# Third q loaded by a GpSimd gather, with eight of its rows loaded by SP

## The chip, the cores and the metric

The kernel runs on one core of a Trainium2 chip. The metric is device time in microseconds; three runs of the kernel before took 166.98 to 167.67 us, with a median of 167.11. One further execution was taken with the hardware profiler, and all rows of the profile are from that one.

## The reference

Linear attention with an ELU feature map, for 32 heads of 2048 rows by 128, all in bf16:

```python
phi_q = jnp.where(q > 0, q + 1, jnp.exp(q)) + 1e-6
phi_k = jnp.where(k > 0, k + 1, jnp.exp(k)) + 1e-6
kv = jnp.einsum("bhsd,bhse->bhde", phi_k, v)
z = jnp.einsum("bhsd->bhd", phi_k)
num = jnp.einsum("bhqd,bhde->bhqe", phi_q, kv)
den = jnp.einsum("bhqd,bhd->bhq", phi_q, z)[..., None] + 1e-6
return num / den
```

## The kernel before

The heads are worked through one after the other, each split into parts that overlap with those of its neighbours. A head's k, v and q are each one DMA of 512 KB: 128 partitions, each with 16 consecutive rows (4 KB, called a row of the transfer here). They land in rings of six buffers (`NBI`), and results leave from a ring of ten (`NBO`).

For each head, ACT takes exp of k, and POOL (DVE in the second head) takes relu of k. DVE clips the exp at 1 and adds the epsilon, so that phi is the sum of two tiles; both go into PE's products with v, or are added first for some of the 16 sub-tiles. PE accumulates kv with a column of ones for z. PE transposes q into PSUM, ACT and DVE take exp and relu of it from there, PE multiplies both with kv, and DVE divides and writes bf16. A store of 512 KB follows.

The first head's kv has no loop: PE runs warming products, the transposes of the first q, the first kv, the transposes of the second q and the first part of the second kv, and then enters a hardware loop of 5 turns of 6 heads.

The order on every engine is written out by hand: `Plan.add` (L32) takes an engine, a key and what an operation reads and writes, and an engine's operations are sorted by key (L57). Waits follow from reads and writes. Three rules touch this change:

- An operation that writes an entry waits for the entry's last writer if that is on another engine or is a DMA:

```python
            if w is not None and (w.eng != eng or w.dma):
                op.deps.append(w)
```

- A wait of an operation in PE's loop whose value is the same in every turn is asked once, ahead of the loop (L173 to L176, L195).
- SP's waits stand in its own order, so that what comes later on SP comes after them.

Loads are issued by SP (`load`, L376), with keys six heads ahead of use. The first ones are k0, q0, v0, k1, q1, v1, k2, q2, then a wait for v0, and k3, v2, k4, q3 and on. `late` (L597) gives the stores keys that move further behind the loads as the heads go on.

`SLOW` (L252) names one head, the fourth from the end, and partitions 16 to 19 and 48 to 51. That head's result is stored in two ways. POOL issues one indirect DMA with a list of row numbers (`row_sb`, made on DVE at L327 to L334); for those eight partitions the number is beyond the bound, so that they are left out. SP stores them as 3, 1, 3 and 1 rows (L604).

Of the kernel before, what the change touches and what calls it, by code (L numbers as in the profile page):

```python
# [6 lines left out]
ALU = mybir.AluOpType  # L7
P = 128
# [223 lines left out]
def bass_standalone__linear_attn_elu__prompt_kernel(  # L232
# [8 lines left out]
    NT = 16  # L241
    NH = B * H
    bf16 = mybir.dt.bfloat16
    fp32 = mybir.dt.float32
    NBI = 6
    NBO = 10
# [3 lines left out]
    HALF = NT * P // 2  # L250
    LAST = NH - 1
    SLOW = {LAST - 3: (16, 48)}  # L252

    ADD = (10, 11, 12, 13, 14)
    EVEN, ODD = tuple(range(0, NT, 2)), tuple(range(1, NT, 2))
# [4 lines left out]
    qf = q.rearrange("b h s d -> (b h) s d")  # L260
# [4 lines left out]
    with ExitStack() as es:  # L265
        def sb(name, shape, dt):
            return es.enter_context(nc.sbuf_tensor(name, shape, dt))
# [3 lines left out]
        q_sb = sb("q_sb", [P, NBI, NT * D], bf16)  # L271
# [10 lines left out]
        ident = sb("ident", [P, P], bf16)  # L282
        ones_sb = sb("ones_sb", [P, 1], bf16)
        first_sb = sb("first_sb", [1, 64], bf16)
        part_sb = sb("part_sb", [P, 1], mybir.dt.int32)
        off_sb = sb("off_sb", [P, len(SLOW)], fp32)
        num_sb = sb("num_sb", [P, len(SLOW)], fp32)
        row_sb = sb("row_sb", [P, len(SLOW)], mybir.dt.int32)

        xT_ps = es.enter_context(nc.psum_tensor("xT_ps", [P, NT * P], bf16))  # L290
        kvz_ps = es.enter_context(nc.psum_tensor("kvz_ps", [P, 512], fp32))
# [6 lines left out]
        def dma_sem(name):  # L298
            return dsems[name]

        for n, c in (("k", NBI), ("q", NBI), ("v", NBI), ("va", 1), ("o", NBO + 1 + len(SLOW))):
            for i in range(c):
                dsems[(n, i)] = es.enter_context(nc.semaphore(f"s_{n}{i}"))

        pl = Plan()

        def rows(x, h):
            return x[h].rearrange("(p j) d -> p (j d)", j=NT)
# [11 lines left out]
               reads=[("id0",)], writes=[("ident",)])  # L320
        pl.add("pool", -7, lambda g: g.memset(_ap(vfull, 0, [[VW, NBI], [1, GAP]]), 1.0), writes=[("vones",)])

        pl.add("pool", -6.9, lambda g: g.iota(part_sb[:], pattern=[[0, 1]], base=0, channel_multiplier=1), writes=[("part",)])
        for i, (h, groups) in enumerate(SLOW.items()):
            off, num, row = off_sb[:, i:i + 1], num_sb[:, i:i + 1], row_sb[:, i:i + 1]
            far = (groups[-1] - groups[0]) / 2
            steps = [lambda d, off=off, m=groups[0] + far + 1.5: d.tensor_scalar(off, part_sb[:], m, None, op0=ALU.subtract),  # L327
                     lambda d, off=off: d.tensor_tensor(out=off, in0=off, in1=off, op=ALU.mult)]
            if far:
                steps += [lambda d, off=off, m=far * far + 4.0: d.tensor_scalar(off, off, m, None, op0=ALU.subtract),  # L330
                          lambda d, off=off: d.tensor_tensor(out=off, in0=off, in1=off, op=ALU.mult)]
            steps += [lambda d, off=off, m=(3.5 * far) ** 2 + 4.0: d.tensor_scalar(off, off, m, float(NH * P), op0=ALU.is_lt, op1=ALU.mult),
                      lambda d, num=num, h=h: d.tensor_scalar(num, part_sb[:], float(h * P), None, op0=ALU.add),
                      lambda d, off=off, num=num, row=row: d.tensor_tensor(out=row, in0=num, in1=off, op=ALU.add)]  # L334
            for n, f in enumerate(steps):
                pl.add("dve", -8.3 + 0.01 * i + 0.001 * n, f, reads=[("part",)] + [("off", i)] * (n > 0), writes=[("off", i), ("row", i)])

        def mm_held(pe, out_ap, rhs, stop, start=False):
            return pe.add_instruction(mybir.InstMatmult(  # L339
                start_tensor_calc=start, stop_tensor_calc=stop, ldweights=False, bass_skip_group_check=True,  # L340
                tile_position=(0, 0), tile_size=(P, P), name=nc.get_next_instruction_name(), engine=mybir.EngineType.PE,
                ins=[pe.lower_ap(rhs), pe.lower_ap(held[0])], outs=[pe.lower_ap(out_ap)]))
# [27 lines left out]
        for h in range(NH):  # L370
# [3 lines left out]
            bi, b2, b3, bo = h % NBI, h % 2, h % 3, h % NBO  # L374

            def load(name, buf, src, key, h=h, bi=bi, after=()):  # L376
                dst, rws = buf[:, bi], rows(src, h)
                if name == "v":
                    dst = v_sb[:, bi, GAP:]
                return pl.add("sp", key, lambda sp: sp.dma_start(dst, rws), writes=[(name, bi)] + ([("vo", bi)] if name == "v" else []),  # L380
                              dma=(name, bi), after=after)
# [2 lines left out]
            this_v = load("v", v_sb, vf, h - NBI - 0.8)  # L384
            if h == 0:
                first_v.append(this_v)
            load("q", q_sb, qf, h - NBI - 0.9)

            pl.add("act", at("ek", -2.8),
                   lambda a, bi=bi, b2=b2: a.activation(ek_sb[:, b2, :], k_sb[:, bi, :], ACT.Exp),  # L390
                   reads=[("k", bi)], writes=[("ek", b2)])
# [8 lines left out]
            else:  # L400
# [4 lines left out]
                   reads=[("ek", b2)], writes=[("emk", b3)], kind="emk")  # L405
# [36 lines left out]
            if h:  # L442
                pl.add("pe", at("kv", -1.2), lambda pe, kv=kv, t=both_of: kv(pe, t, start=True),
                       reads=[("emk", b3), ("rk", b3, 0), ("rk", b3, 1)] + base, writes=[("bankkv",)])
            pl.add("pe", at("kv", -1.199), lambda pe, kv=kv, t=one_of, f=h == 0: kv(pe, t, start=f, stop=f),
                   reads=[("phix" if h == 1 else "phik", b3)] + base + ([] if h else [("first",)]), writes=[("bankkv",)])
            if h:
                pl.add("pool", h + 0.6, lambda g, bi=bi: g.memset(_ap(vfull, bi * VW + GAP + D - 1, [[2 * D, NT // 2], [1, 1]]), 1.0),
                       reads=[("v", bi)], writes=[("vo", bi)], kind="vo")
                pl.add("pe", at("kv2", -0.2985), lambda pe, kv=kv: kv(pe, ODD, stop=True),  # L450
                       reads=[("phik", b3), ("emk", b3), ("rk", b3, 0), ("rk", b3, 1), ("v", bi), ("vo", bi)], writes=[("bankkv",)])
            pl.add("act", at("kvs", -0.95), lambda a, b3=b3: a.activation(kvs_sb[:, b3, :], kvz_ps[:, 0:NC], ACT.Copy),  # L452
                   reads=[("bankkv",)], writes=[("kvs", b3)], kind="kvs")

            def tr(half, bi=bi):
                def f(pe):
                    for j in range(8 * half, 8 * half + 8):
                        last = pe.transpose(xT_ps[:, j * P:(j + 1) * P], q_sb[:, bi, j * P:(j + 1) * P], ident[:])  # L458
                    return last
                return f  # L460

            for half in (0, 1):
                pl.add("pe", h - 1.25 + 0.01 * half, tr(half), reads=[("q", bi), ("ident",)], writes=[("bankx", half)],
                       after=[halves[1]] if h == 1 and half == 0 else ())
            both = [("bankx", 0), ("bankx", 1)]

# [18 lines left out]
            else:  # L485
# [5 lines left out]
                   reads=[("eq", b2, 0), ("eq", b2, 1)], writes=[("emq", b3)], kind="emq")  # L491
# [105 lines left out]
            late = h + 1.0 + 0.18 * h  # L597
            if h in SLOW:
                i = list(SLOW).index(h)
# [3 lines left out]
                    reads=[("row", i)] + [("o", bo, p) for p in ("t", 0, 1, 2, 3, 4)], dma=("o", NBO + 1 + i))  # L603
# [38 lines left out]
```

## Time and profile before

| | |
|---|---|
| median of three runs | 167.11 us (166.98 to 167.67) |
| profiled execution | 167.06 us |
| its span, first to last instruction | 165.8 us |
| PE, DVE, ACT busy | 156.2, 153.2, 155.0 us |
| POOL busy | 107.6 us |
| DMA | 67.25 MB in 18605 packets, mean 406 GB/s |
| queue q1 (SP's) | 18448 packets, 66.63 MB |
| queue q0 (POOL's) | 144 packets, 0.49 MB |
| granted TensorE clock | 0.992 |

The page gives the busy time of each engine; the span cut into 40 slices of 4.15 us, each with a busy share in tenths; the DMA queues; and groups of instructions. A row of a timeline has start, length, engine, line and operation, and in brackets the idle time before it with what ended it. PEld is PE's weight load, SPq an issue on SP's queue. An issue's landing is the time at which all 16 DMA engines have counted its semaphore up.

### The profile page before, as it was taken

How to read it: one execution, taken by the hardware profiler on the slowest of the kernel's cores; microseconds unless marked ns; L12 is line 12 of the kernel's file. 1: busy time of each engine (PE TensorE's matmuls, PEld its weight loads, DVE VectorE, ACT ScalarE, POOL GpSimd, SP SyncE). 2: the span in 40 equal slices, each digit the busy share in tenths (PEclk: the TensorE clock that was granted, in tenths of full speed). 3: DMA queues.
4: the chain of work that ended last, by engine and by line, in shares of the span. 5: the costliest groups of instructions: out<-in, count | busy, mean ns of one | idle time of the engine just before them, and what ended most of it. 6: DMA issues, size and time to landing. Idle time of an engine off the chain costs nothing.

```text
span 165.8 us, 6280 instructions
## 1 busy us (share of the span) xinstructions
PE 156.2 (94%) x2819; PEld 145.7 (88%) x2453; DVE 153.2 (92%) x277; ACT 155.0 (94%) x143; POOL 107.6 (65%) x130
## 2 busy tenths in 40 slices
PE   7799999999999999999999999999999999999970
PEld 0379899999999999899999989999998999999960
DVE  3588999999999999999999999999999999999992
ACT  3989999999999999999999999999999999999681
POOL 2406688776767887676778767676887767678510
PEclk9999999999999999999999999999999999999996
DMA  5999999999999999999999999999999999999986
GB/s 192 409 416 420 414 421 414 397 390 407 421 417 422 416 420 420 419 420 416 420 419 420 418 421 416 419 420 420 418 420 419 421 419 420 418 419 419 418 348 259
DMA packets 18605, 67.25 MB, mean 406 GB/s; under 512 B 2082, under 2 KB 2210, under 8 KB 18594
## 3 DMA queue, kind: packets, MB, share of 16 engines
q1 hardware_dynamic: 18448, 66.63, 99.2%
q0 software_dynamic: 144, 0.49, 0.7%
q8 instruction: 5, 0.08, 0.2%
q14 instruction: 6, 0.05, 0.1%
q10 hardware_dynamic: 2, 0.00, 0.0%
HBM read 50.33 MB, written 16.81 MB: 405 GB/s over the span
## 4 chain that ended last, share of the span: by engine, by line
DVE 59%; PE 17%; POOL 12%; ACT 6%; issue 3%; DMA 2%; DVEq 0%
DVE o_sb L546 20%; POOL rk_sb L412 12%; DVE rq_sb L478 11%; DVE emk_sb L404 10%; DVE emq_sb L490 10%; PE kvz_ps L435 6%; PE o_ps L505 5%; PE o_ps L506 5%; ACT ek_sb L390 3%; DVE rden_sb L534 3%; DVE o_sb L539 3%; ACT eq_sb L469 2%; DMA k_sb<-in_k_dram 2%; DVE den_sb L528 2%; DVE rk_sb L412 1%
## 5 line engine op out<-in xcount | busy, mean ns | idle before, releaser
L435 PE MATMUL kvz_ps<-v_sb,rk_sb 128*128 128x129 bf16 (+1 forms) x512 | 67.0, 220 | 2.9 <-POOL rk_sb L412 1.2
L546 DVE TENSOR_TENSOR o_sb<-o_ps,rden_sb 128x768 bf16<-128x768 f32 (+2 forms) x62 | 67.9, 1135 | 0.0
L412 POOL TENSOR_TENSOR rk_sb<-rk_sb,emk_sb 128x640 bf16<-128x640 bf16 x30 | 41.9, 1396 | 39.6 <-DVE emq_sb L490 38.3
L394 POOL TENSOR_SCALAR rk_sb<-k_sb 128x1024 bf16<-128x1024 bf16 (+1 forms) x60 | 64.1, 1069 | 2.5 <-DMA k_sb<-in_k_dram 2.5
L505 PE MATMUL o_ps<-kvs_sb,emq_sb 128*128 128x129 bf16 (+1 forms) x536 | 65.2, 217 | 0.0
L506 PE MATMUL o_ps<-kvs_sb,rq_sb 128*128 128x129 bf16 (+1 forms) x536 | 64.4, 217 | 0.0
L469 ACT ACTIVATE eq_sb<-xT_ps 128x2048 bf16<-128x2048 bf16 (+1 forms) x33 | 60.1, 1823 | 2.7 <-PE xT_ps L458 2.7
L390 ACT ACTIVATE ek_sb<-k_sb 128x2048 bf16<-128x2048 bf16 x32 | 61.0, 1908 | 1.6 <-DMA k_sb<-in_k_dram 1.6
L435 PE MATMUL kvz_ps<-v_sb,emk_sb 128*128 128x129 bf16 (+1 forms) x338 | 53.3, 221 | 0.0
L435 PEld LDWEIGHTS kvz_ps<-v_sb,rk_sb 128*128 128x128 bf16 x512 | 46.1, 98 | 7.7 <-POOL rk_sb L412 3.1
L505 PEld LDWEIGHTS o_ps<-kvs_sb,emq_sb 128*128 128x128 bf16 x536 | 51.2, 98 | 0.8 <-issue 0.5
L506 PEld LDWEIGHTS o_ps<-kvs_sb,rq_sb 128*128 128x128 bf16 x536 | 51.3, 98 | 0.0
L458 PE MATMUL xT_ps<-ident,q_sb 128*128 128x128 bf16 x512 | 34.1, 220 | 0.5 <-DMA q_sb<-in_q_dram 0.5
L458 PEld LDWEIGHTS xT_ps<-ident,q_sb 128*128 128x128 bf16 x512 | 30.2, 98 | 4.8 <-DMA q_sb<-in_q_dram 4.3
L435 PEld LDWEIGHTS kvz_ps<-v_sb,emk_sb 128*128 128x128 bf16 x338 | 32.5, 98 | 0.3 <-DVE emk_sb L404 0.2
L339 PE MATMUL kvz_ps<-ones_sb,rk_sb 128*128 128x1 bf16 x232 | 31.3, 165 | 0.0
L476 ACT ACTIVATE rq_sb<-xT_ps 128x1024 bf16<-128x1024 bf16 x30 | 30.9, 1031 | 0.0
L404 DVE TENSOR_SCALAR emk_sb<-ek_sb 128x2048 bf16<-128x2048 bf16 x32 | 22.0, 689 | 3.0 <-ACT ek_sb L390 3.0
L478 DVE TENSOR_SCALAR rq_sb<-xT_ps 128x1024 bf16<-128x1024 bf16 x34 | 23.3, 689 | 1.5 <-ACT eq_sb L469 1.5
L490 DVE TENSOR_SCALAR emq_sb<-eq_sb 128x2048 bf16<-128x2048 bf16 x32 | 21.9, 684 | 0.0
L339 PE MATMUL kvz_ps<-ones_sb,emk_sb 128*128 128x1 bf16 x121 | 19.9, 166 | 0.0
L452 ACT ACTIVATE kvs_sb<-kvz_ps 128x129 bf16<-128x129 f32 x32 | 9.0, 282 | 1.5 <-PE kvz_ps L435 0.9
(37 smaller groups left out, 51.6 us busy)
## 6 DMA issues: line engine op xcount, KB each, us to landing
k_sb<-in_k_dram SPq DMA_DIRECT2D x32, 512.0 KB, 14.9
q_sb<-in_q_dram SPq DMA_DIRECT2D x32, 512.0 KB, 15.1
v_sb<-in_v_dram SPq DMA_DIRECT2D x32, 512.0 KB, 15.1
out_dram<-o_sb SPq DMA_DIRECT2D x30, 512.0 KB, 15.4
out_dram<-o_sb SPq DMA_DIRECT2D x1, 288.0 KB, 3.3
out_dram<-o_sb SPq DMA_DIRECT2D x1, 224.0 KB, 3.1
out_dram<-o_sb SPq DMA_DIRECT2D x2, 12.0 KB
out_dram<-o_sb SPq DMA_DIRECT2D x2, 4.0 KB
```

What stands on the lines that cost most here:

```text
L339: return pe.add_instruction(mybir.InstMatmult(start_tensor_calc=start, stop_tensor_calc=stop, ldweights=False, bass_skip_group_check=True, ...
L390: lambda a, bi=bi, b2=b2: a.activation(ek_sb[:, b2, :], k_sb[:, bi, :], ACT.Exp),
L394: pl.add(eng, key, lambda e: e.tensor_scalar(rk_sb[:, b3, c], k_sb[:, bi, c], BIG, 0.0, op0=ALU.min, op1=ALU.max), reads=[("k", bi)] + ([( ...
L404: lambda d, b2=b2, b3=b3: d.tensor_scalar(emk_sb[:, b3, :], ek_sb[:, b2, :], 1.0, EPS, op0=ALU.min, op1=ALU.add),
L412: return e.tensor_tensor(out=a, in0=a, in1=b, op=ALU.add)
L435: last = pe.matmul(kvz_ps[:, 1 - l:NC], lhsT=w, rhs=v_sb[:, bi, c - l:c + D], start=first, stop=fin, skip_group_check=True)
L458: last = pe.transpose(xT_ps[:, j * P:(j + 1) * P], q_sb[:, bi, j * P:(j + 1) * P], ident[:])
L469: halves[part] = pl.add("act", key, lambda a: a.activation(eq_sb[:, b2, c], xT_ps[:, c], ACT.Exp), reads=both[part:part + 1] or both, writ ...
L478: f = lambda d: d.tensor_scalar(rq_sb[:, b3, c], xT_ps[:, c], 0.0, None, op0=ALU.max)
L505: pe.matmul(o_ap, lhsT=emq_sb[:, b3, t * P:(t + 1) * P], rhs=kvs_sb[:, b3, c0:c1], start=True, stop=False)
L506: return pe.matmul(o_ap, lhsT=rq_sb[:, b3, t * P:(t + 1) * P], rhs=kvs_sb[:, b3, c0:c1], start=False, stop=True)
L546: pl.add("dve", key, lambda d: d.tensor_tensor(out=o_sb[:, bo, 3 * g0:3 * g1, :].rearrange("p (a b) d -> p a b d", b=3), in0=_ap(full, bas ...
```

## The change

The third head's q (`EARLY = 2`) is no longer one DMA on SP. SP loads its partitions 16 to 18, 19, and 48 to 51 as three DMAs, with a key that puts them ahead of the second q. POOL then issues one indirect DMA that gathers the other 120 rows by a list. The list is the scatter's, moved by a whole number of heads with one more operation on DVE, so that the eight rows stay out of bounds. The gather waits for the three loads; the transposes of the third q, and of every later q in the same buffer, also read the gather's entry `qa`.

```diff
+    EARLY = 2
...
-        row_sb = sb("row_sb", [P, len(SLOW)], mybir.dt.int32)
+        row_sb = sb("row_sb", [P, len(SLOW) + 1], mybir.dt.int32)
...
+        first = next(iter(SLOW))
+        pl.add("dve", -8.2, lambda d: d.tensor_scalar(row_sb[:, len(SLOW):len(SLOW) + 1], row_sb[:, 0:1], float((EARLY - first) * P), None, op0=ALU.add),
+               reads=[("row", 0)], writes=[("row", len(SLOW))])
...
-            load("q", q_sb, qf, h - NBI - 0.9)
+            if h == EARLY:
+                few = []
+                for p0, p1 in ((SLOW[first][0], SLOW[first][0] + 3), (SLOW[first][0] + 3, SLOW[first][0] + 4), (SLOW[first][1], SLOW[first][1] + 4)):
+                    few.append(pl.add("sp", 0.05 - NBI, lambda sp, p0=p0, p1=p1, bi=bi, h=h: sp.dma_start(q_sb[p0:p1, bi], rows(qf, h)[p0:p1]),
+                           writes=[("q", bi)], dma=("q", bi)))
+                pl.add("pool", 0.5, lambda g, bi=bi: g.indirect_dma_start(
+                    q_sb[:, bi], None, q.rearrange("b h (p j) d -> (b h p) (j d)", j=NT),
+                    bass.IndirectOffsetOnAxis(ap=row_sb[:, len(SLOW):len(SLOW) + 1], axis=0), bounds_check=NH * P - 1, oob_is_err=False),
+                    reads=[("row", len(SLOW))], writes=[("qa", bi)], dma=("qa", 0), after=few)
+            else:
+                load("q", q_sb, qf, h - NBI - 0.9)
...
-                pl.add("pe", h - 1.25 + 0.01 * half, tr(half), reads=[("q", bi), ("ident",)], writes=[("bankx", half)],
+                pl.add("pe", h - 1.25 + 0.01 * half, tr(half), reads=[("q", bi), ("ident",)] + [("qa", bi)] * (bi == EARLY), writes=[("bankx", half)],
```

More of the change, by code (lines that the diff above doesn't have):

```diff
@@ L299, in dma_sem @@
             return dsems[name]
-        for n, c in (("k", NBI), ("q", NBI), ("v", NBI), ("va", 1), ("o", NBO + 1 + len(SLOW))):
+        for n, c in (("k", NBI), ("q", NBI), ("v", NBI), ("va", 1), ("qa", 1), ("o", NBO + 1 + len(SLOW))):
             for i in range(c):
```

## The prediction

> **What bounds the kernel now.** I read the page's parts 1 to 3 first, then the stages, then the first 17 us on SP, PE and ACT, and last the completion records of the stores.
>
> Part 1 has PE, DVE and ACT at 92 to 94%. Part 2 has the DMA engines as full as they are:
>
> ```profile
> DMA  5999999999999999999999999999999999999986
> GB/s 192 409 416 420 414 421 414 397 390 407 421 417 422 416 420 420 419 420 416 420 419 420 418 421 416 419 420 420 418 420 419 421 419 420 418 419 419 418 348 259
> ```
>
> After the first slice they never rest. The stage table (columns: stage, length, busy time with count of PE, PEld, DVE, ACT, POOL, granted clock, DMA share, GB/s) says the same and shows where the share falls:
>
> ```profile
> 80.00:120.00 40.00, 39.55 (x742) 38.38 (x652) 39.30 (x68) 39.58 (x36) 28.95 (x35) 1.00 1.03 419
> 120.00:156.00 36.00, 35.48 (x669) 34.34 (x578) 35.30 (x62) 34.05 (x29) 25.55 (x29) 1.00 1.03 419
> 156.00:160.00 4.00, 3.88 (x72) 3.71 (x71) 3.86 (x9) 3.71 (x11) 1.27 (x2) 1.00 1.01 407
> 160.00:162.00 2.00, 0.78 (x14) 0.60 (x11) 1.90 (x10) 1.87 (x8) 0.00 (x0) 1.00 0.75 299
> ```
>
> 67.25 MB at 419 GB/s are 160.5 us of a 165.8 us span. So there are two bounds side by side: the chain of engines, and the DMA engines. Which ends last is read from the final store, issued at 162.57. Its 16 completion counts (one for each DMA engine, from the trace's completion records) land at 164.45 to 164.62 for twelve engines, then 164.88, 165.22, 165.47 and 165.72. The twelve had run dry and waited for compute (the 0.75 above); the last four still had a backlog. The span ends with the last of them. **An idle stretch of a backlogged DMA engine therefore lengthens the kernel one for one.** Compute has 1.1 us to spare there (165.72 less 164.62).
>
> **What the change does at the start.** Issues of SP in before, with time, length and operation:
>
> ```profile
> 0.74 0.38 SPq L380 DMA_DIRECT2D k_sb<-in_k_dram  x1
> 1.18 0.42 SPq L380 DMA_DIRECT2D q_sb<-in_q_dram  x1
> 1.65 0.42 SPq L380 DMA_DIRECT2D v_sb<-in_v_dram  x1
> 2.12 0.43 SPq L380 DMA_DIRECT2D k_sb<-in_k_dram  x1
> 2.59 0.49 SPq L380 DMA_DIRECT2D q_sb<-in_q_dram  x1
> ...
> 4.09 0.45 SPq L380 DMA_DIRECT2D q_sb<-in_q_dram  x1
> 6.97 0.33 SPq L380 DMA_DIRECT2D k_sb<-in_k_dram  x1
> ```
>
> Eight loads are queued by 4.5 us. By issue-to-landing times of 3.4, 4.2, 5.3, 6.1 and 6.9 us the first five land at 4.1, 5.4, 7.0, 8.2 and 9.5: in order of issue, 1.25 us apart. That queue covers the wait for the first v that ends at 6.97.
>
> In the changed program the fifth to seventh issues are the 3, 1 and 4 rows. All three write the same buffer entry, and the planner makes a DMA that writes what another DMA wrote wait for it (L44 to L48). Its listing of SP has that wait ahead of the 1 row and ahead of the 4 rows; the second q (L385) comes after them:
>
> ```
> 3 L385 DMACopy k_sb<-in_k_dram 128x2048
> 4 L395 DMACopy q_sb<-in_q_dram 3x2048
> 5 L395 DMACopy q_sb<-in_q_dram 1x2048 [waits s_q2]
> 6 L395 DMACopy q_sb<-in_q_dram 4x2048 [waits s_q2]
> 7 L385 DMACopy q_sb<-in_q_dram 128x2048
> ```
>
> So SP stands still twice, and the second q, second v, third k and all later loads are behind it.
>
> **The sum, step by step.**
> 1. The 3 rows are issued at 2.59, behind the second k, whose counts land from 7.67 to 8.2. One row more on three engines takes 0.16 us (1.25 us for 8 rows): 7.8 to 8.4, taken 8.0. SP wakes within 0.02 (v at 6.95, issue at 6.97).
> 2. The 1 row is issued at 8.02, when the queue has just run dry (the 512th row ends at 7.51 in the packet records). No row shows one 4 KB row from an empty queue. Below: the 64 bytes that ACT loads (issue 0.74, landing 1.91), 1.17 us. Above: the first k, 3.40 us for 8 rows an engine, less 1.25 for the rows: 2.15. I take 1.6, near the middle, since the row is a single packet but as far from a warm queue as the first k: 9.6.
> 3. The 4 rows are issued at 9.62 without holding the second q, which goes one issue pitch (0.47) later: 10.1, between 9.5 and 11.05 by the bounds above.
> 4. The second q lands after 3.40 us at most (the first k's own time) and 2.42 at least (1.17 + 1.25). Taken 2.9: 13.0 instead of 9.45. **The DMA stream is 3.55 us late**, with ends 2.4 and 5.0.
>
> The Trainium skill (DMA: Bandwidth & Descriptors, Anatomy of one DMA) puts a fixed cost of about 2.0 us on a DMA, mostly the receipt of the last write, fitted on GpSimd's path. The trace's smallest load shows 1.17. By the page step 2 would end 0.4 later and the time be 170.8, an estimate that the sum does not use.
>
> Beside this the other edits are small:
> - The list: one more 128x1 operation on DVE. Its kin take 0.15 to 0.16 us at 1.8 to 3.1 us, and DVE idles until 6.11: nothing. Without that cover it costs 0.2.
> - The relief: 8 rows leave one DMA engine. That rows 16 to 19 and 48 to 51 are one engine's is borne out at the end of before: the slowest count is 1.7 us behind the next (161.88 and 160.20) for the store ahead of the scatter that leaves those rows out, and 0.25 behind (165.72 and 165.47) after it. 8 rows are 1.25 us, but the next engine ends 0.25 earlier, so **the relief is worth 0.25**, unless that next engine gets the extra row of L395 (0.09 then).
> - The gather on POOL: POOL waits for the three loads, issues, and then does the memset that waited until 12.42 in before. Its issue is bounded by the scatter's 1.14 us. POOL's relu for the third head, behind it in the queue, waits for the third k anyway and has 1.3 us of idle after it.
> - PE: the changed listing asks for the gather at the loop's entry, ahead of the first numerators, not ahead of the third transposes. In before PE enters at 12.2. What is queued behind: numerators, the rest of kv, and the transposes that ACT's exp at 16.67 waits for.
>
> ```profile
> 10.05 1.05 PE L458 MATMUL xT_ps<-ident,q_sb 128*128 128x128 bf16 x16
> 11.14 1.88 ACT L469 ACTIVATE eq_sb<-xT_ps 128x2048 bf16<-128x2048 bf16 x1 [0.82 <-PE xT_ps L458]
> 12.91 1.90 ACT L390 ACTIVATE ek_sb<-k_sb 128x2048 bf16<-128x2048 bf16 x1
> ```
>
> Compute moves too: the second transposes start at 13.0 instead of 10.05, so the exp behind them (ACT idles only 0.82 ahead of it) is 2.9 late. The gather: the 4 rows land near 11.2, and the scatter's landing took 3.9 (first engine) to 6.5 us (last), so PE enters at 15.1 to 17.7. From entry to the third exp PE needs 3.7 us, and 16.67 - 3.7 is 12.95, or 12.8 through ACT's chain: compute is 2.3 to 4.9 late. Steady rounds have DVE at 98% and give nothing back. Compute decides the end only above 3.55 - 0.25 + 1.1 = 4.4, so the DMA stream is the later one.
>
> Sum: 3.55 - 0.25 = **+3.3 us**, span 165.8 to 169.1. The profiled execution took 167.06, which is 1.3 over its span and 0.05 under the median of 167.11. **Forecast 170.4 us.**
>
> **Rivals.**
> - *The gather decides.* Where it lands 6.5 us after its issue, PE enters at 17.7, compute is 4.9 late and the last counts land at 164.62 + 4.9 = 169.5: 170.9 us. DVE is busy from 9.2 to 11.9 in before; if POOL cannot write its list of transfers beside it, 0.7 to 1.0 more, 171.9. The Trainium skill states such a lock (SBUF — State Buffer, SBUF: two separate sides); the scatter's 1.14 us beside a DVE relu of 0.68 does not show it. Against: the 6.5 belongs to an engine 2 us behind, and none is so late at 11 us. Chance 0.20.
> - *Compute hides part.* If the late engines catch up (the 0.75 at 160 to 162 shows that most can), compute alone decides, 3.0 late: 164.62 + 3.0 = 167.6, or 169.0 us. Against: four engines never ran dry. Chance 0.14.
> - *Not slower.* If the small loads landed under cover of queued loads, with the second q issued before 6.6 (7.5 less 0.9 to the first packet), only the relief would stay: 166.8 us. For: they use 1 to 4 engines. Against: loads land in order of issue, and the small stores of the end, issued from 152.1, landed at 158.3 to 158.8, behind the store issued before them. Chance 0.04.
>
> The forecast itself has 0.60, and 0.02 is left for what I have not thought of.
>
> **The numbers.** Range: 2.4 and 5.0 less 0.25, so 169.2 to 171.8; this holds the gather's case at 170.9 and leaves out part of the second rival. A measurement of this kernel tells 0.5% (0.84 us) from no change. Slower by more: 0.95; within: 0.03; faster: 0.02, all from the last rival and the rest.
>
> **What would show it.** SP: 3 rows near 2.6, 1 row near 8.0, 4 rows near 9.6, the second q near 10.1, with two waits for q_sb of some 5 and 1.6 us. The third slice of GB/s falls from 416 to about 150. PE waits for q_sb at the second transposes, to about 13. The gather's issue stands near 11.2. In the final store the slowest count is no longer alone. I am wrong if SP issues the second q before 6.6, if the third slice stays near 400, or if PE's wait at the loop's entry runs past 17.2: then the gather decides.

## The result, and the profile after

| | before | changed |
|---|---|---|
| time, median of 6 runs each on the same chip, us | 167.29 (166.98 to 168.57) | 175.58 (175.29 to 176.98) |
| ratio | | 1.0498, 95% interval [1.0448, 1.0548] |
| profiled execution: time, span, us | 167.06, 165.8 | 175.82, 174.5 |

The change makes the kernel slower by 8.3 us. The forecast was 170.4 with a range to 171.8: the direction is right, the size is not.

Part 2 of the changed kernel's page first (40 slices of 4.4 us; the clock that TensorE was granted, the DMA engines' busy tenths, GB/s):

```profile
PEclk9996579999999999999999999999999999999999
DMA  5659999999999999999999999999999999999356
GB/s 215 269 185 394 412 416 417 415 362 416 414 417 420 419 420 419 418 418 420 418 420 421 420 419 419 417 418 420 420 421 420 420 421 420 421 417 416 127 229 250
```

Two things are to be seen besides the hole of the third slice, which the forecast expected (185; it said about 150). The clock falls to 0.5 in the fifth slice. And the last three slices are no longer full: in before the DMA engines were busy to the end, here they run dry from about 162 us on. The end has changed hands, from DMA to the engines.

SP's rows answer to those of before, then POOL's row with the gather, and the landing of the two indirect DMAs (last column: us from issue to landing):

```profile
2.59 7.12 SPq L395 DMA_DIRECT2D q_sb<-in_q_dram  x3
9.76 0.36 SPq L385 DMA_DIRECT2D q_sb<-in_q_dram  x1
```

```profile
12.28 1.20 POOL L397 DMA_INDIRECT q_sb<-in_q_dram,row_sb  x1 [6.36 <-issue]
```

```profile
q_sb<-in_q_dram,row_sb POOLq DMA_INDIRECT x1, 8.6
out_dram<-o_sb,row_sb POOLq DMA_INDIRECT x1, 5.1
```

The three small loads hold SP until the second q goes out at 9.76 (forecast 10.1); by the completion records it lands at 12.99 (forecast 13.0). So SP's part came as worked out. The gather did not: the last small rows land at 11.27, POOL issues 1.0 us after that, and the rows need 8.6 us, longer than any scatter here does (at most 7.4, in experiment 11). What this does to PE, in its waits and at the row where it enters the loop:

```profile
PE o_ps L520 <- DMA q_sb<-in_q_dram,row_sb: 5.3, 1, 5.3
```

```profile
21.06 0.28 PE L520 MATMUL o_ps<-kvs_sb,emq_sb 128*128 128x129 bf16 x1 [5.29 <-DMA q_sb<-in_q_dram,row_sb]
```

In before PE did not wait there:

```profile
12.22 0.22 PE L505 MATMUL o_ps<-kvs_sb,emq_sb 128*128 128x129 bf16 x1
```

So the first numerator (a product of the first q with kv) starts 8.8 us later than in before. ACT shows what follows. Its rows for the second head's kvs (kv as ACT copies it out of PSUM), the exp of the fourth k and the exp of the third q, in before and then in the changed kernel:

```profile
14.71 0.27 ACT L452 ACTIVATE kvs_sb<-kvz_ps 128x129 bf16<-128x129 f32 x1
14.87 1.91 ACT L390 ACTIVATE ek_sb<-k_sb 128x2048 bf16<-128x2048 bf16 x1
16.67 1.88 ACT L469 ACTIVATE eq_sb<-xT_ps 128x2048 bf16<-128x2048 bf16 x1
```

```profile
24.31 0.28 ACT L467 ACTIVATE kvs_sb<-kvz_ps 128x129 bf16<-128x129 f32 x1 [5.65 <-PE kvz_ps L450]
24.49 1.90 ACT L405 ACTIVATE ek_sb<-k_sb 128x2048 bf16<-128x2048 bf16 x1
26.30 1.88 ACT L484 ACTIVATE eq_sb<-xT_ps 128x2048 bf16<-128x2048 bf16 x1
```

Compute is 9.6 us late here, and 9.75 at the last DVE operation, which ends at 172.29 instead of 162.54 (before, then changed):

```profile
161.99 0.55 DVE L546 TENSOR_TENSOR o_sb<-o_ps,rden_sb 128x384 bf16<-128x384 f32 x1
```

```profile
171.74 0.55 DVE L561 TENSOR_TENSOR o_sb<-o_ps,rden_sb 128x384 bf16<-128x384 f32 x1
```

The span grows by 8.7, as about 1 us comes back at the end: all 16 counts of the last store land together, 174.22 to 174.44, without the backlog that put the last one at 165.72 in before. The stages show where PE stood and how it came back (length, busy time with count of PE, PEld, DVE, ACT, POOL, granted clock, DMA share, GB/s):

```profile
12.00:16.00 4.00, 2.48 (x34) 2.11 (x26) 0.00 (x0) 1.83 (x1) 1.33 (x2) 0.76 1.00 397
16.00:20.00 4.00, 0.00 (x0) 0.00 (x0) 3.70 (x4) 1.95 (x2) 1.95 (x2) 0.50 1.01 404
20.00:24.00 4.00, 2.94 (x30) 2.95 (x31) 0.00 (x0) 0.00 (x0) 2.33 (x2) 0.50 1.03 421
...
160.00:164.00 4.00, 4.00 (x78) 3.90 (x69) 3.94 (x7) 2.69 (x3) 2.66 (x5) 1.00 0.70 277
```

From 16 to 20 PE does nothing at all, and from 21 to 24 it works at half clock. It was not the wait for the gather that brought the clock down: by the trace's clock record it is 0.50 from 14.06 to 24.30, so it fell before that wait began (15.78), after PE had stood from 10.02 to 13.08 for the second q. The long wait kept it down. At 160 to 164 PE and DVE are full and the DMA share is 0.70.

One figure worked out from the packets helps with all that follows: the **stream's lag**, how much later than in before the DMA engines have moved as many bytes. In the changed kernel it is 4.1 us at 20 us and 4.2 us at 40, 80, 120 and 155 us. So the forecast's stall is there, 4.2 us for 3.55, and stays. But the end is 8.7 us late, and it is not the stream that ends last.

### The profile page after: what moved, and what is told of

Same layout as the page of the kernel before. It is cut to its first block, busy times and chain, and to the rows that moved or that the text cites. A ratio compares the mean times of both kernels' runs of the same rounds, so it can differ in the third digit from the quotient of the medians.

```text
span 174.5 us, 6293 instructions
## 1 busy us (share of the span) xinstructions
PE 157.2 (90%) x2819; PEld 147.2 (84%) x2453; DVE 154.5 (89%) x278; ACT 155.2 (89%) x143; POOL 108.7 (62%) x131
## 4 chain that ended last, share of the span: by engine, by line
DVE 56%; PE 17%; POOL 11%; DMA 10%; issue 3%; SPq 1%; POOLq 0%
DVE o_sb L561 20%; POOL rk_sb L427 11%; DVE rq_sb L493 10%; DVE emq_sb L505 9%; DVE emk_sb L419 9%; PE kvz_ps L450 6%; PE o_ps L520 6%; PE o_ps L521 5%; DMA q_sb<-in_q_dram 5%; DMA q_sb<-in_q_dram,row_sb 5%; DVE rden_sb L549 3%; DVE o_sb L554 3%; DVE den_sb L543 2%; SPq L385 1%; PE kvz_ps L344 0%
## 5 line engine op out<-in xcount | busy, mean ns | idle before, releaser
L520 PE MATMUL o_ps<-kvs_sb,emq_sb 128*128 128x129 bf16 (+1 forms) x536 | 66.1, 219 | 5.3 <-DMA q_sb<-in_q_dram,row_sb 5.3
L450 PE MATMUL kvz_ps<-v_sb,rk_sb 128*128 128x129 bf16 (+1 forms) x512 | 67.9, 223 | 2.6 <-DVE rk_sb L427 0.8
L521 PE MATMUL o_ps<-kvs_sb,rq_sb 128*128 128x129 bf16 (+1 forms) x536 | 65.1, 219 | 0.0
L450 PE MATMUL kvz_ps<-v_sb,emk_sb 128*128 128x129 bf16 (+1 forms) x338 | 54.0, 223 | 0.2 <-issue 0.2
L450 PEld LDWEIGHTS kvz_ps<-v_sb,rk_sb 128*128 128x128 bf16 x512 | 46.8, 99 | 7.2 <-POOL rk_sb L427 2.6
L505 DVE TENSOR_SCALAR emq_sb<-eq_sb 128x2048 bf16<-128x2048 bf16 x32 | 23.1, 721 | 0.0
```

Source lines behind the costliest of these rows:

```text
L450: last = pe.matmul(kvz_ps[:, 1 - l:NC], lhsT=w, rhs=v_sb[:, bi, c - l:c + D], start=first, stop=fin, skip_group_check=True)
L505: lambda d, b2=b2, b3=b3: d.tensor_scalar(emq_sb[:, b3, :], eq_sb[:, b2, :], 1.0, EPS, op0=ALU.min, op1=ALU.add),
L520: pe.matmul(o_ap, lhsT=emq_sb[:, b3, t * P:(t + 1) * P], rhs=kvs_sb[:, b3, c0:c1], start=True, stop=False)
L521: return pe.matmul(o_ap, lhsT=rq_sb[:, b3, t * P:(t + 1) * P], rhs=kvs_sb[:, b3, c0:c1], start=False, stop=True)
```

## The experiments

Theory A is the forecast's: SP stands still, the DMA stream is late, and the late stream sets the end. Theory B: the gather's landing sets it, through PE's wait at the loop's entry and the half clock after it; SP's stall lies beneath. Every kernel here is the changed one with the edit shown, unless said otherwise.

**1. No chain** (the three loads count on semaphores of their own).

```diff
+                    own = ("qs", len(few) - 1) if few else ("q", bi)
-                           writes=[("q", bi)], dma=("q", bi)))
+                           writes=[own], dma=own))
```

> The three small loads count on semaphores of their own, so that SP issues them one behind the other and waits for none; the gather still waits for all three. Theory A, the forecast's: SP's stall is what costs, the second q lands at about 10 us instead of 12.99 and nearly all of the loss is gone, about 168 us. Theory B: the end is set by the gather's last landing at PE's loop entry and by the half clock behind it. Its issue moves from 12.3 to about 9.4 to 10 us, its last landing from 20.8 to about 17.5 to 18.5, PE's first numerator from 21.1 to about 18 to 18.7, and the time falls by the same 2.5 to 3 us, to about 172.5 to 173 us.

174.01 us, ratio 1.0396 [1.0357, 1.0435]. SP, POOL and PE:

```profile
2.59 0.93 SPq L396 DMA_DIRECT2D q_sb<-in_q_dram  x3
```

```profile
11.28 1.20 POOL L398 DMA_INDIRECT q_sb<-in_q_dram,row_sb  x1 [5.10 <-DMA q_sb<-in_q_dram]
```

```profile
19.32 0.28 PE L521 MATMUL o_ps<-kvs_sb,emq_sb 128*128 128x129 bf16 x1 [5.78 <-DMA q_sb<-in_q_dram,row_sb]
```

SP waits for nothing, the stream's lag falls to 0.2 us, and still 6.4 us of loss remain: **theory A falls.** PE enters 7.1 us late and the span (172.8) is 7.0 us longer. B was 1.0 to 1.5 us too hopeful: the gather is issued at 11.28, not 9.4 to 10. The small rows queue behind the first four loads, the last of which lands at 9.43, and their own last count is at 10.29; POOL takes another 1.0 us from there to the issue.

**2. Chain only** (the whole third q by SP, no gather).

```diff
-                pl.add("pool", 0.5, lambda g, bi=bi: g.indirect_dma_start(
...
+                load("q", q_sb, qf, h - NBI - 0.9)
```

> The three small loads and SP's two waits stay, the gather is gone: SP loads the whole third q as before the change, on a semaphore of its own, so that the loop's entry waits for no gather. Both theories price SP's stall alone here: the forecast's sum of 3.3 us less the 120 rows that move a second time, about 170.3 us if the late loads set the end (A). Theory B has no claim of its own on the stall: 167.5 to 170.5 us; its claim is that the rest, 5 us or more of the 8.3, is the gather's, so that nothing above 171 us is seen here.

173.22 us, ratio 1.0339 [1.0275, 1.0403]: more than either theory allowed. The stream's lag is 4.2 us, as in the changed kernel, but the span is 6.7 us longer. ACT's rows for the third and fourth k:

```profile
17.16 1.91 ACT L402 ACTIVATE ek_sb<-k_sb 128x2048 bf16<-128x2048 bf16 x1 [0.92 <-DMA k_sb<-in_k_dram]
...
21.22 1.91 ACT L402 ACTIVATE ek_sb<-k_sb 128x2048 bf16<-128x2048 bf16 x1 [1.98 <-DMA k_sb<-in_k_dram]
```

In before the fourth k had landed at 14.46 and ACT took it at 14.87 (the row shown above), without a wait: 0.4 us of lead. Here its last count is at 21.19 and ACT starts at 21.22, 6.35 us late. The load is later than the stream (6.7 for 4.2) because its 16 counts are 3.1 us apart, 0.56 in before: fifteen of them are in by 19.46, and one DMA engine follows at 21.19. A fetch of 16 KB of instructions holds one DMA engine for 0.95 us from 18.55; that it is the same engine is not shown. An exp waits for the last DMA engine, the lag is an average over all. So the stall costs compute its lead over the loads and the spread on top, and compute decides without any gather. This is read from the rows; no run varied the lead alone.

**3. Wait at use** (the loop's first turn written out, so that the wait for the gather stands at the third transposes).

```diff
-        pl.emit(nc, sems, dma_sem, (("num", 0), ("num", LAST - 1), 5))
+        pl.emit(nc, sems, dma_sem, (("num", 6), ("num", LAST - 1), 4))
```

> The loop takes its last four turns only and the first is written out, so that the wait for the gather stands at the third head's transposes instead of at the loop's entry. Theory B: PE does the second head's first products meanwhile, about 4 us of work of the 5.3 us wait, and keeps its clock; about 171.5 us. Theory A: the wait costs nothing beside the late loads, and the time stays within 0.5 us of 175.6. The code is longer by five heads' instructions, which may cost some fetches of instructions more.

172.87 us, ratio 1.0316 [1.0283, 1.0349], 2.7 us better than the changed kernel although SP stalls no less (the stream's lag is 5.2 us in this profile).

The third transposes, in before and here:

```profile
14.84 1.06 PE L458 MATMUL xT_ps<-ident,q_sb 128*128 128x128 bf16 x16
```

```profile
23.05 1.05 PE L473 MATMUL xT_ps<-ident,q_sb 128*128 128x128 bf16 x16 [3.06 <-DMA q_sb<-in_q_dram,row_sb]
```

The wait has moved and shrunk from 5.3 to 3.1 us. A is refuted again, B is right in sign and 1.4 us too hopeful. The time is close to that of experiment 2, which has no gather. What the gather adds at its use beside the stall can't be read from that, as the two profiles have different lags.

**4 and 5. Warming products** ahead of the loop's entry, 28 and then 12.

```diff
-        WARM = ((-9, 9), (-1.22, 4), (-0.27, 3))
+        WARM = ((-9, 9), (-1.22, 4), (-0.27, 3), (0.5, 28))
```

> 28 warming products stand on PE's queue ahead of the loop's entry, where it idles for the gather. If the half clock after the idle wait is part of the loss (B): with the clock kept up, the numerators after 21 us have their usual pitch, kvs comes about 1.3 us earlier than 24.3 us, and the time falls to about 174.2 us. Theory A, or a clock that doesn't matter: 175.6 us, no change.

176.42 us, ratio 1.0513 [1.0467, 1.0558]: no gain, as 28 were too many; PE was still at them when the gather landed, and its first numerators stood at 24.03. But from there to kvs (25.84) it took 1.81 us, not 3.25. Hence 12 of them:

> 12 warming products instead of 28 ahead of the loop's entry, so that they end before the gather lands at 20.8 to 21 us. If the half clock of PE behind its idle wait is a part of the loss, kvs comes 1.8 us after the first numerator as with 28 of them, not 3.25 us, and the time is 174.2 us, 1.4 below the changed kernel. Rival: the 1.4 us are taken back later, and 175.6 us stay.

174.85 us, ratio 1.0447 [1.0399, 1.0494]. PE's entry and ACT's kvs, then the stage ahead of the entry:

```profile
21.32 0.23 PE L520 MATMUL o_ps<-kvs_sb,emq_sb 128*128 128x129 bf16 x1 [1.57 <-DMA q_sb<-in_q_dram,row_sb]
```

```profile
23.14 0.28 ACT L467 ACTIVATE kvs_sb<-kvz_ps 128x129 bf16<-128x129 f32 x1 [4.23 <-PE kvz_ps L450]
```

```profile
16.00:20.00 4.00, 3.75 (x22) 0.51 (x4) 2.78 (x4) 2.91 (x2) 2.01 (x2) 0.79 1.02 411
20.00:24.00 4.00, 2.68 (x49) 2.69 (x50) 0.07 (x1) 0.86 (x2) 2.40 (x2) 1.00 1.03 420
```

With the clock up, kvs comes 1.82 us after the entry: the half clock costs 1.4 us there, and the span is 1.0 us shorter although PE enters 0.26 us later. In the time it is 0.7 us and the two intervals overlap, so the time alone does not settle it; the rows do.

**6. An empty indirect DMA first** (same list, a bound that leaves every row out).

```diff
+                pl.add("pool", 0.4, lambda g: g.indirect_dma_start(
+                    dry_sb[:], None, q.rearrange("b h (p j) d -> (b h p) (j d)", j=NT),
+                    ..., bounds_check=0, oob_is_err=False),
+                    reads=[("row", len(SLOW))], writes=[("dry",)], dma=("dry", 0))
```

> POOL issues one more indirect DMA ahead of the gather, at about 6 us, with the same list and a bound that leaves every row out, so that it moves no row; its destination is a tile of its own. The gather's first packet stood 4.4 to 5.0 us after its issue in the four kernels so far, the scatter's 2.3 us, and the scatter is the program's second indirect DMA there, but its first in the kernel before, where it has 2.26 us as well. Theory cold start: the first indirect DMA of a program, or one that the rest of POOL's work has not preceded, is slow; the gather's first packet comes 2.3 us after its issue, PE's loop entry at about 19 us, time about 173.5 us. Theory direction or place: a gather into the chip's memory is slow whatever went before; 4.4 us and 175.6 us again.

176.88 us, ratio 1.0550 [1.0489, 1.0611].

```profile
dry_sb<-in_q_dram,row_sb POOLq DMA_INDIRECT x1, 3.1
q_sb<-in_q_dram,row_sb POOLq DMA_INDIRECT x1, 8.5
```

The gather, now second, is as slow: issue 13.26, first packet 17.76 by the packet records, 4.5 us later. No cold start.

**7. Gather alone** (SP's second q waits for the gather too; one execution).

```diff
+                second.deps.append(alone)
```

> The changed kernel, but SP's second q also waits for the gather, so that the gather runs beside no load. Which of two makes its first packet come 4.4 us after the issue: if the queued loads do, it comes after 2.2 to 2.4 us and all rows land within about 2 us more, 17 to 17.5 us instead of 20.8 at a like issue; if a gather from the chip's memory is slow by itself, it is 4.4 us again. The total is no matter here; SP's stall grows by 6 us or more.

```profile
q_sb<-in_q_dram,row_sb POOLq DMA_INDIRECT x1, 4.1
```

Issue 12.74, first packet 14.57, last landing 16.84. With no load beside it the gather starts after 1.8 us and lands after 4.1; beside the loads that SP puts out from 9.76 on it is 4.4 and 8.6. **The loads beside it cost the gather 4.5 us**, 2.6 of them ahead of its first packet (16.71 in the changed kernel) and 1.9 behind it. While its rows run, from 17 to 19 us, the changed kernel's packet records have 93 of them beside 106 of the loads, about an even share. The lock that the forecast's first rival named is not the cause: in the changed kernel DVE ran nothing from 11.67 to 16.15 us, while POOL's instruction stood from 12.28 to 13.48. (The time here, 177.44 us, follows SP's longer stall: the stream's lag is 10.2 us, and the span 10.4 us longer.)

**8. Small loads only** (no waits, into a tile of their own; whole third q by SP, no gather).

```diff
-                    few.append(pl.add("sp", 0.05 - NBI, lambda sp, ...: sp.dma_start(q_sb[p0:p1, bi], rows(qf, h)[p0:p1]),
-                           writes=[("q", bi)], dma=("q", bi)))
+                    own = ("qs", len(few))
+                    few.append(pl.add("sp", 0.05 - NBI, lambda sp, ...: sp.dma_start(dry_sb[p0:p1], rows(qf, h)[p0:p1]),
+                           writes=[own], dma=own))
```

> The three small loads alone, at the same place on SP, on semaphores of their own and into a tile of their own, so that SP waits for none; the whole third q comes by SP as before the change, and there is no gather. Beside the chain-only kernel (173.2 us) the two waits on SP are all that is gone. If the waits are the stall's price (forecast's step and theory B alike): about 167.5 us, the DMA stream within 0.6 us of the kernel before. If small transfers at this place cost by themselves: 169 us or more.

168.41 us, ratio 1.0021 [0.9978, 1.0063]. The loads by themselves cost nothing that can be told from no change; against experiment 2, SP's two waits cost about 5 us.

**9. Both edits** (1 and 3 together).

> Small loads without SP's waits, and the wait for the gather at the third head's transposes instead of at the loop's entry. Theory B (the gather's landing is a bound of its own): the landing stays at 19 to 19.5 us, the third transposes come at 19.3 us instead of 14.84, and of these 4.5 us about 2.7 to 3.5 reach the end, 170 to 171 us. Theory A: 167.5 us, as nothing is left of SP's stall.

171.13 us, ratio 1.0209 [1.0141, 1.0278].

```profile
19.60 1.05 PE L474 MATMUL xT_ps<-ident,q_sb 128*128 128x128 bf16 x16 [3.43 <-DMA q_sb<-in_q_dram,row_sb]
```

The stream's lag is 0.4 us; the third transposes are 4.8 us late (14.84 in before), the span 4.2. The gather is a bound of its own at its use too: the third q is due at 14.84, and a gather issued at 10.53 beside the loads lands at 19.47.

**10. Both edits, later head** (`EARLY = 5`).

> As the kernel with both edits, but the gather serves the sixth q (EARLY = 5) instead of the third: it is issued and lands at the same times, and its transposes are due at about 29 us. Theory B: nothing waits for it, and the time comes back to that of the kernel before, 167.0 to 167.8 us. Rival: the 120 rows of the gather cost DMA time of their own beside the loads or put engines out of step, and 169 us or more are left.

167.92 us, ratio 1.0003 [0.9978, 1.0029]. All the loss is gone, and nothing is won.

**11. The kernel before, first turn written out** (the edit of experiment 3 alone).

> The kernel before, with the loop of four turns and the first turn written out: what the longer code costs by itself in the kernels that move the wait. 167.0 to 167.9 us if it is nothing or a few fetches of instructions; 168.5 us or more would mean that those kernels owe more than a microsecond to it.

167.93 us, ratio 1.0016 [0.9994, 1.0039]: the longer code of experiments 3, 9 and 10 costs 0.7 us at most.

The runs side by side. The start is that of the operation whose wait decides, less its start in before:

| kernel | stream's lag at 140 us | late start | span, less before's |
|---|---|---|---|
| changed | 4.2 | PE's entry 8.8 | 8.7 |
| 1 no chain | 0.2 | PE's entry 7.1 | 7.0 |
| 2 chain only | 4.2 | exp of fourth k 6.35 | 6.7 |
| 3 wait at use | 5.2 | third transposes 8.2 | 6.4 |
| 4 warm, 28 | 4.8 | PE's entry 11.8 | 10.3 |
| 5 warm, 12 | 4.9 | PE's entry 9.1 | 7.7 |
| 6 empty one first | 5.5 | PE's entry 9.8 | 9.5 |
| 7 gather alone | 10.2 | second transposes 10.0 | 10.4 |
| 9 both edits | 0.4 | third transposes 4.8 | 4.2 |

The end goes with the late start to within 0.6 us, not with the lag, in six of the nine. In experiments 3, 4 and 5 it is 1.4 to 1.8 us less, and these are the three whose clock is 1.00 behind the wait; the other six have a stretch of 0.50 beside or behind it. That fits the 1.4 us of experiment 5. The stall alone costs 3.4%, the gather at the loop's entry alone 4.0%, both 5.0%: they lie beside each other, and the later one decides; both cost more than the gather alone, as with the stall the gather is issued 1.0 us later and takes 0.7 us longer to land.

## Why the forecast was wrong, point by point

- Steps 1 to 3, SP's issues: right. 1 row at 8.13 (8.02 forecast), 4 rows at 9.47 (9.62), second q at 9.76 (10.1).
- Step 4: the second q at 12.99 (13.0). That it fits to 0.01 is luck: its issue came 0.3 us earlier than forecast and its landing took 3.2 us, not 2.9. That the stream is late by as much (3.55) was 0.65 short, between the ends given.
- Small edits: the list cost nothing seen. The relief of 0.25 us can't be told: experiment 10 has it and stands between -0.4 and +0.5 us.
- **The step that failed is the gather's: "the scatter's landing took 3.9 (first engine) to 6.5 us (last), so PE enters at 15.1 to 17.7".** PE entered at 21.06. Of the 3.4 us beyond the upper end, 1.1 is the issue (12.28, not 11.2), as POOL took 1.0 us from the landing to the issue, a term that the forecast put at nothing; 2.1 is the landing, 8.6 for 6.5, and 0.2 stands between the last landing and PE's first product. The forecast took the scatter for an upper bound, on the ground that no engine is 2 us behind at 11 us. Experiment 7 shows another reason, the loads beside it. The scatter had none: in before the last load had landed at 150.8, the scatter was issued at 156.90, and what ran beside it were stores. So "the DMA stream is the later one" failed with it: compute was 9.75 us late, far above the 4.4 from which it decides. Either half of the change alone is past the range's upper end of 171.8: the gather without the stall (174.01) and the stall without the gather (173.22).
- From entry to the third exp the forecast took before's pace, less its slack. PE worked at half clock there, 1.4 us more by experiment 5. The Trainium skill (TensorE: Matmul & The Clock Gate, Part 1) has the array fall to half clock after a window of about 3.4 us without work. The traces agree on the step, as the stretches at half clock are 3.41, 6.83 or 10.24 us long, but not on the idle window: from 10.65 to 14.06, ahead of the fall, PE was busy for 0.98 us, and in experiment 8 for 1.71 us (7.29 to 10.71). The forecast had this first wait, "PE waits for q_sb at the second transposes, to about 13"; it asked how long PE waits, not what the wait does to it.
- That compute decides only above 4.4 us was right as a rule, but both branches were above it. Even without the gather (experiment 2) compute decides, as the loads of k have 0.4 us of lead to lose, where 4.2 would be needed to hide the stall. The forecast moved the second transposes by 2.9 us and left the loads of k where they were.
- The rivals: "the gather decides", held at 0.20, was the mechanism, 4.7 us too small (170.9). "Not slower" needed the second q issued before 6.6; experiment 10, which meets it (3.57) with the gather out of the way, can't be told from no change. "Compute hides part", held at 0.14, had its condition come true: the late DMA engines did catch up, as the last store's 16 counts show, and compute alone decided. Its 3.0 us for compute were 9.75, and its time of 169.0 was 6.6 too small.
- The forecast named its own refutation, PE's wait past 17.2, and that is what came.

## What to carry to other kernels

Price a transfer that is waited for beside the transfers that run with it: a row from another direction or another load is no upper bound for it. The few tenths of a microsecond that each load is ahead of its use belong in the sum. Look in the changed listing for where a wait really stands: moving one from the loop's entry to its use was worth 2.7 us, and with that and no wait on SP, giving the gather to a head that is due later brought back the rest. Two bounds that are a microsecond apart do not add: when a start moves by more than that, follow the later start.

## What the runs showed of the chip

- A gather of 120 rows of 4 KB: first packet 1.8 us after the issue and all landed after 4.1 with no load beside it (experiment 7); 4.4 to 5.0 and 7.8 to 10.4 beside the loads. The scatter has 2.26 us to its first packet in before, beside 401 GB/s of stores. No run has a gather beside stores or a scatter beside loads, so whether the direction or the loads make the difference stays open. The Trainium skill (DMA: Bandwidth & Descriptors, Queues, rings and completion order) has an engine finish a whole packet of one queue, some 9 to 17 descriptors, before it turns to the next; 16 rows of 0.157 us are 2.5 us, an estimate by that page, near the 2.6 us that the gather lost, but the scatter, which had a queue of stores beside it, does not bear it out.
- An indirect DMA that moves no row lands after 3.1 us (experiment 6).
- From the last count of the small loads to POOL's issue of the gather it took 0.99 to 1.01 us in eight of the nine kernels that have one, and 0.81 in experiment 6, where another indirect DMA went ahead. SP issued 0.02 us after the count it waited for (6.95 and 6.97 in before).
- PE's clock changed in steps of 3.41 us. Counted over all profiles up to some 10 us from their ends, it fell after each of the 11 steps at full clock with 1.71 us of PE work or less, and after none of the 553 with 1.81 us or more; it came back after the 11 steps at half clock with 2.88 us or more, and not after the 8 with 2.73 or less. In the changed kernel it was 0.50 for 10.24 us; with 12 products put into the wait, PE was busy from 13.78 to 19.75 and it was 0.50 for 3.41 us (14.30 to 17.71).
